# Sparse attention and expert attention on one core: loop order written by hand, against an order from a list scheduler at build time

## The chip, the cores and the metric

The kernel runs on one core of a Trainium2 chip. The metric is the time of one execution on the device in microseconds (us). A profiled execution has a span besides, from its first to its last instruction.

## The reference

Two stages follow each other, on 4 batches of 768 positions. The first is attention with 8 heads of 64, in which a position sees the last 96 positions and the first 8, with a bias by head and distance. The second takes its output x (512 features) through 4 experts, each a causal attention of its own with 64 features, and adds the two experts that a router picks for each position.

```python
# stage 1: q, k, v (4, 8, 768, 64)
scores = q @ k.T / 8 - slope[h] * dist        # dist = 96 for the 8 global columns outside the window
a = softmax(where(is_global | is_local, scores, -1e9));  x = concat_heads(a @ v)
# stage 2
logits = x @ w_gate                            # (4, 768, 4); the two largest, softmax over them: w
for e in range(4):
    ye = softmax(causal(x @ wq[e] @ (x @ wk[e]).T / 8)) @ (x @ wv[e]) @ wo[e]
    out += (e is one of the two) * w[e] * ye
```

## The kernel before

Work is cut into 24 units: 4 batches (b) by 6 row tiles of 128 positions (ri). Softmax is done without subtracting the maximum; the mask and bias of stage 1 are a factor M on the exponentials, and the sums come from a column of ones beside V. At the end a count over all reciprocals of sums decides whether a general path (a second, slow version of everything, `general_path`) has to run; with these inputs it is jumped over.

The steps of one unit u, in the order of its data:

- `load` (L274 to L282): q, k and v of the unit by three transfers on SP's queue, rows of 64 f32. `cast` (L397): q and k together, then v, to f16 on POOL.
- `transposes` (L404): 8 transposes on PE, copied out by DVE as qkT (L412). For ri = 0 POOL copies the 8 global keys into KG (L420).
- `scores1`, twice (hf = 0, 1): scores on PE (L433), exponential on ACT (L437), mask product on DVE (L439), all of 4 heads x 128 keys x (128 + 96) queries.
- `scores_g`: scores of the global keys (L449), exponential on ACT (L452). `values1`, twice: products with V and VG on PE (L460 to L468), reciprocal and scaling on DVE (L471, L474).
- `xpose`: x transposed on PE (L481), copied by DVE (L483).
- `proj_qk`: 16 matmuls (L492), copied by DVE (L494). `proj_v`: V of the experts and the gate's 4 logits in one tile (L501); V copied by ACT (L503); the router on DVE and ACT: copy of the logits, the two largest, subtraction, exponential on ACT (L511), choice, sum (L505 to L516).
- `scores2`, one to three chunks: scores on PE (L537), exponential on ACT (L540); POOL blanks the causal triangle of the first chunk (L542).
- `values2`: products on PE (L556), normalisation with the router's weights on DVE (L559 to L565). `zpose`, `output`: transposes, the product with wo on PE (L583), copy by ACT (L586), transfer to out on SP's queue (L587).

Each step runs on one fixed engine. The loop (L600 to L634) issues in pass i the steps of three units, i, i-1 and i-2, in an order written out by hand; each engine runs its own instructions in that order. Loads run three units ahead. PSUM has two tiles of two banks for scores and four of one bank for all else. Most SBUF tiles have two or three buffers.

Ahead of the loop, ACT's queue issues all transfers of weights (L291 to L296), 15 of them, with rows of 64 f32 for wq, wk and wv, and 32 of the 8 global rows of v (L300). Then POOL and DVE build masks and constants, and ACT the factors M0 and M (L333, L336). All stand on ACT's queue behind the issues.

Of the kernel before, what the change touches and what calls it, by code (L numbers as in the profile page):

```python
# [8 lines left out]
F32 = mybir.dt.float32  # L9
# [6 lines left out]
HUGE = 1.0e30  # L16
P = 128
N_G, N_L = 8, 96

# [217 lines left out]

@with_exitstack
def kernel(
# [17 lines left out]
    DV = Dh + 1  # L257

# [4 lines left out]
    ring2 = main.enter_context(tc.tile_pool(name="ring2", bufs=2))  # L263
    ring3 = main.enter_context(tc.tile_pool(name="ring3", bufs=3))
# [5 lines left out]


    raw = {}

    def load(u):  # L274
        b, ri = divmod(u, n_rt)
        rows = slice(ri * P, (ri + 1) * P)
        qk32 = ring3.tile([P, 2, H, Dh], F32, name="qk32")
        v32 = ring3.tile([P, H, Dh], F32, name="v32")
        nc.sync.dma_start(qk32[:, 0, :, :], q[b, :, rows, :].rearrange("h s d -> s h d"))
        nc.sync.dma_start(qk32[:, 1, :, :], k[b, :, rows, :].rearrange("h s d -> s h d"))  # L280
        nc.sync.dma_start(v32[:, :, :], v[b, :, rows, :].rearrange("h s d -> s h d"))
        raw[u] = (qk32, v32)  # L282

    load(0)
    load(1)


    w32 = const.tile([P, 4, nko, E, Hd], F32, name="w32")
    for n, w in enumerate((moe_wq, moe_wk, moe_wv)):
        for e in range(E):  # L290
            nc.scalar.dma_start(w32[:, n, :, e, :], w[e].rearrange("(ko kp) d -> kp ko d", kp=P))  # L291
    wo32 = const.tile([P, E // 2, Dm], F32, name="wo32")
    for p2 in range(E // 2):
        nc.scalar.dma_start(wo32[:, p2, :], moe_wo[2 * p2:2 * p2 + 2].rearrange("e d n -> (e d) n"))
    wg32 = const.tile([P, nko, E], F32, name="wg32")
    nc.scalar.dma_start(wg32[:, :, :], moe_w_gate.rearrange("(ko kp) e -> kp ko e", kp=P))  # L296
    vg32 = const.tile([N_G * H, B, Dh], F32, name="vg32")
    for b in range(B):
        for h in range(H):
            nc.scalar.dma_start(vg32[h * N_G:(h + 1) * N_G, b, :], v[b, h, 0:N_G, :])  # L300


    ident = const.tile([P, P], FH, name="ident")
    make_identity(nc, ident[:, :])


    di = const.tile([P, P + N_L], I32, name="di")
    pool.iota(di[:, 0:P], pattern=[[1, P]], channel_multiplier=-1, base=0)
    pool.iota(di[:, P:P + N_L], pattern=[[1, N_L]], channel_multiplier=-1, base=P)
    d = const.tile([P, P + N_L], F32, name="d")  # L310
    dve.tensor_copy(d[:, :], di[:, :])

    pool.affine_select(out=d[:, 0:P], in_=d[:, 0:P], pattern=[[1, P]], channel_multiplier=-1,
                       base=0, compare_op=Alu.is_ge, fill=HUGE)

    pool.affine_select(out=d[:, 0:P], in_=d[:, 0:P], pattern=[[-1, P]], channel_multiplier=1,
                       base=N_L - 1, compare_op=Alu.is_ge, fill=HUGE)
    pool.affine_select(out=d[:, P:P + N_L], in_=d[:, P:P + N_L], pattern=[[-1, N_L]],
                       channel_multiplier=1, base=N_L - 1 - P, compare_op=Alu.is_ge, fill=HUGE)

    dg = const.tile([P, P], F32, name="dg")
    pool.memset(dg[:, :], float(N_L))
    pool.affine_select(out=dg[:, :], in_=dg[:, :], pattern=[[0, P]], channel_multiplier=-1,
                       base=N_G - 1, compare_op=Alu.is_ge, fill=HUGE)
    d0 = const.tile([P, P], F32, name="d0")
    dve.tensor_tensor(d0[:, :], d[:, 0:P], dg[:, :], op=Alu.min)

# [3 lines left out]
    for h in range(H):  # L331
        hf, pr, par = h // 4, (h // 2) % 2, h % 2
        act.activation(M0[:, hf, par, pr, :], d0[:, :], func=Exp, scale=-slopes[h])  # L333
    for h in range(H):
        hf, pr, par = h // 4, (h // 2) % 2, h % 2
        act.activation(M[:, hf, par, pr, :], d[:, :], func=Exp, scale=-slopes[h])  # L336


    bm = const.tile([P, H], F32, name="bm")
    bmd = const.tile([P, H], F32, name="bmd")  # L340
    pool.memset(bmd[:, :], 0.0)

    pool.affine_select(out=bmd[:, :], in_=bmd[:, :], pattern=[[-N_G, H]], channel_multiplier=1,
                       base=0, compare_op=Alu.is_ge, fill=HUGE)
    pool.affine_select(out=bmd[:, :], in_=bmd[:, :], pattern=[[N_G, H]], channel_multiplier=-1,
                       base=N_G - 1, compare_op=Alu.is_ge, fill=HUGE)
    for h in range(H):
        dve.tensor_scalar(bm[:, h:h + 1], bmd[:, h:h + 1], -1.0, -slopes[h] * N_L,
                          op0=Alu.mult, op1=Alu.add)
    act.activation(bm[:, :], bm[:, :], func=Exp)  # L350
    VG = const.tile([P, B, H, DV], FH, name="VG")
    pool.memset(VG[:, :, :, :], 0.0)
    NL = N_G * H

    def make_vg(b):
        pool.tensor_tensor(
            VG[0:NL, b, :, 0:Dh], vg32[:, b, :].unsqueeze(1).to_broadcast([NL, H, Dh]),
            bm[0:NL, :].unsqueeze(2).to_broadcast([NL, H, Dh]), op=Alu.mult)
        pool.tensor_copy(VG[0:NL, b, :, Dh:DV], bm[0:NL, :].unsqueeze(2))

    KG = [const.tile([P, H // 2, P], FH, name=f"KG{i}") for i in range(2)]
    for t in KG:
        pool.memset(t[:, :, :], 0.0)
    NV = 4
    V1 = [const.tile([P, H, DV + 1], FH, name=f"V1_{i}") for i in range(NV)]
    for t in V1:
        pool.memset(t[:, :, Dh:DV], 1.0)
    V2 = [const.tile([P, n_rt, E, DV + 1], FH, name=f"V2_{i}") for i in range(2)]
    for t in V2:
        pool.memset(t[:, :, :, Hd:DV], 1.0)  # L370
    QK2 = [const.tile([P, n_rt, 4, P], FH, name=f"QK2_{i}") for i in range(2)]

    NA = 4
    A1 = [const.tile([P, 2, 2, 2 * P], FH, name=f"A1_{i}") for i in range(NA)]
    for t in A1:
        pool.memset(t[:, :, :, P + N_L:2 * P], 0.0)
    NLG = 4
    LG = [const.tile([P, 8], F32, name=f"LG{i}") for i in range(NLG)]
    for t in LG:
        pool.memset(t[:, E:8], -HUGE)  # L380
    rall = const.tile([P, NU, H + E], F32, name="rall")
    ones = const.tile([P, 1], F32, name="ones")
    pool.memset(ones[:, :], 1.0)

    wqk = const.tile([P, nko, 4, P], FH, name="wqk")
    wvg = const.tile([P, nko, E * Hd + E], FH, name="wvg")
    wo = const.tile([P, E // 2, Dm], FH, name="wo")
    dve.tensor_copy(wqk[:, :, 0:2, :].rearrange("p k a (e d) -> p k (a e) d", d=Hd), w32[:, 0, :, :, :])
    dve.tensor_copy(wqk[:, :, 2:4, :].rearrange("p k a (e d) -> p k (a e) d", d=Hd), w32[:, 1, :, :, :])
    act.copy(wvg[:, :, 0:E * Hd].rearrange("p k (e d) -> p k e d", d=Hd), w32[:, 2, :, :, :])  # L390
    dve.tensor_copy(wvg[:, :, E * Hd:], wg32[:, :, :])
    act.copy(wo[:, :, :], wo32[:, :, :])


    T = {}

    def cast(u):  # L397
        qk32, v32 = raw.pop(u)
        qk16 = ring2.tile([P, 2, H, Dh], FH, name="qk16")
        pool.tensor_copy(qk16[:, :, :, :], qk32[:, :, :, :])  # L400
        pool.tensor_copy(V1[u % NV][:, :, 0:Dh], v32[:, :, :])
        T[u, "qk16"] = qk16

    def transposes(u):  # L404
        b, ri = divmod(u, n_rt)
        qk16 = T.pop((u, "qk16"))
        ps = wtile([P, 2, H // 2, P], FH, "tq")
# [277 lines left out]
```

## Time and profile before

| what | value |
|---|---|
| time, median of 3 runs | 254.3 us (252.79 to 254.62) |
| profiled execution: its time | 254.38 us |
| profiled execution: its span | 252.7 us |
| mean granted clock of PE | 0.934 |
| busy: PE, DVE, ACT, POOL | 158.5, 142.8, 117.4, 69.1 us |
| transfers | 27.81 MB, mean 110 GB/s |

The span is what the profile's rows cover; 1.7 us of the execution lie around it. Busy times of an engine count overlapping instructions once. A step's row gives its engine, line, operation and the program's names for output and input; what stands in brackets behind a row is the idle time of the engine ahead of it and what ended that.

### The profile page before, as it was taken

To read this page: it belongs to the slowest core of one execution; us is meant where nothing else is said; L and a number is where in the kernel's file an instruction comes from. 1 tells how busy PE (TensorE), PEld (TensorE's weight loads), DVE (VectorE), ACT (ScalarE), POOL (GpSimd) and SP (SyncE) were. 2 spreads that over 40 slices of the span, in tenths; PEclk is the share of its full clock that TensorE was granted. 3 is DMA by queue.
4 is the path that set the end of the run, shared out by engine and by line. 5 is a ranking of instruction groups with operands and counts; after the bars stand their busy time and mean duration, and the time that the engine had idled before them with its cause. 6 is when DMAs were issued, how large, how long until landed. Compare 5 with 4: busy or idle time off the path is not lost. (4 is left out here: it accounts for less than half of the span.)

```text
span 252.7 us, 6001 instructions
## 1 busy us (share of the span) xinstructions
PE 158.5 (63%) x2362; PEld 112.2 (44%) x2362; DVE 142.8 (56%) x473; ACT 117.4 (46%) x208; POOL 69.1 (27%) x146
## 2 busy tenths in 40 slices
PE   0020000677787788789788777887878877777740
PEld 0010000545565556556656545655556645555420
DVE  0140002467677786767777687667876767674430
ACT  0000084135466756445557744466666545565510
POOL 4530009730233341332035330233242331011100
PEclk9999999999999999977999999799999979996755
DMA  8999200860654677644756557734777430111011
GB/s 157 218 245 171 49 3 1 154 97 0 159 131 99 118 166 167 145 110 87 166 129 147 119 112 169 166 93 104 143 169 166 115 96 3 43 44 45 0 42 56
DMA packets 86037, 27.81 MB, mean 110 GB/s; under 512 B 82672, under 2 KB 82672, under 8 KB 86000
## 3 DMA queue, kind: packets, MB, share of 16 engines
q1 hardware_dynamic: 78336, 25.17, 45.8%
q10 hardware_dynamic: 7664, 2.17, 4.7%
q8 instruction: 20, 0.33, 0.6%
q14 instruction: 17, 0.14, 0.2%
HBM read 21.05 MB, written 6.29 MB: 108 GB/s over the span
## 5 line engine op out<-in xcount | busy, mean ns | idle before, releaser
L437 ACT ACTIVATE A<-sc 128x896 f16<-128x896 f32 (+1 forms) x48 | 41.5, 866 | 35.9 <-PE sc L433 35.9
L439 DVE TENSOR_TENSOR A<-A,M 128x896 f16<-128x896 f16 (+1 forms) x48 | 29.8, 623 | 45.9 <-ACT A L437 45.9
L542 POOL TENSOR_SCALAR_AFFINE_SELECT A<-A 128x512 f16<-128x512 f16 x24 | 15.3, 637 | 139.8 <-ACT A L540 139.8
L540 ACT ACTIVATE A<-s 128x1024 f16<-128x1024 f32 (+1 forms) x48 | 43.3, 917 | 0.3
L410 PE MATMUL tq<-ident,qk 128*128 128x128 f16 x192 | 16.0, 231 | 42.4 <-POOL qk L400 42.4
L492 PE MATMUL pq<-xT,wqk 128*128 128x128 f16 x384 | 29.3, 237 | 4.9 <-DVE xT L483 4.8
L410 PEld LDWEIGHTS <-qk 128*128 128x128 f16 x192 | 11.7, 103 | 45.1 <-POOL qk L400 42.7
L492 PEld LDWEIGHTS <-wqk 128*128 128x128 f16 x384 | 27.0, 107 | 7.0 <-issue 5.2
L400 POOL CAST qk<-qk 128x1024 f16<-128x1024 f32 x24 | 24.9, 1036 | 0.3
L511 ACT ACTIVATE el<-dl 128x4 f32<-128x4 f32 x24 | 5.0, 207 | 37.6 <-DVE dl L509 37.6
L474 DVE TENSOR_TENSOR x<-z,rall 128x256 f16<-128x256 f32 x48 | 20.4, 424 | 1.6
L586 ACT COPY o_sb<-po 128x512 f32<-128x512 f32 x24 | 14.1, 586 | 13.9 <-PE po L583 9.3
L460 PE MATMUL z<-VG,ag 128*128 128x260 f16 x40 | 11.3, 282 | 13.9 <-ACT ag L452 13.9
L583 PE MATMUL po<-wo,zT 128*128 128x512 f16 x48 | 15.5, 405 | 6.5 <-DVE zT L575 6.5
L433 PE MATMUL sc<-qkT 64*128 64x128 f16 (+1 forms) x352 | 18.3, 226 | 1.2 <-DVE qkT L412 1.2
L412 DVE COPY qkT<-tq 128x1024 f16<-128x1024 f16 x24 | 16.4, 682 | 4.4 <-PE tq L410 4.4
L494 DVE CAST QK<-pq 128x512 f16<-128x512 f32 x24 | 16.5, 686 | 3.2 <-PE pq L492 3.2
L537 PE MATMUL s<-QK 64*128 64x128 f16 x336 | 18.2, 223 | 0.0
L481 PE MATMUL tx<-ident,x 128*128 128x128 f16 x96 | 14.4, 240 | 5.4 <-DVE x L474 5.3
L465 PE MATMUL z<-V,A 128*128 128x65 f16 x192 | 17.4, 196 | 0.0
L556 PE MATMUL z<-V,A 128*128 128x65 f16 x336 | 16.0, 201 | 1.3 <-ACT A L540 1.2
L333 ACT ACT_TABLE_LOAD x1 | 1.3, 1283 | 32.6 <-DMA vg<-in_v_dram 32.6
(73 smaller groups left out, 262.9 us busy)
## 6 DMA issues: line engine op xcount, KB each, us to landing
qk<-in_q_dram SPq DMA_DIRECT2D x24, 256.0 KB
qk<-in_k_dram SPq DMA_DIRECT2D x24, 256.0 KB
v<-in_v_dram SPq DMA_DIRECT2D x24, 256.0 KB
out_dram<-o_sb SPq DMA_DIRECT2D x24, 256.0 KB
w<-in_moe_wq_dram ACTq DMA_DIRECT2D x4, 128.0 KB
w<-in_moe_wk_dram ACTq DMA_DIRECT2D x4, 128.0 KB
w<-in_moe_wv_dram ACTq DMA_DIRECT2D x4, 128.0 KB
wo<-in_moe_wo_dram ACTq DMA_DIRECT2D x2, 256.0 KB
```

Source lines behind the costliest of these rows:

```text
L400: pool.tensor_copy(qk16[:, :, :, :], qk32[:, :, :, :])
L410: nc.tensor.transpose(ps[:, s, p, :], qk16[:, s, 2 * p:2 * p + 2, :], ident[:, :])
L412: dve.tensor_copy(qkT[:, :, :, :], ps[:, :, :, :])
L433: mm(o, lhsT=kt[L, 1, p, :], rhs=qkT[L, 0, p, 0:N_L] if prev else qkT[L, 0, p, :], start=True, stop=True)
L437: act.activation(A[:, :, :, 0:w], sc[:, :, :, 0:w], func=Exp, scale=scale1)
L439: dve.tensor_tensor(A[:, :, :, 0:w], A[:, :, :, 0:w], m, op=Alu.mult)
L465: mm(z[:, h % 4, :], lhsT=A[:, par, pr, 0:P], rhs=V1[u % NV][:, h, 0:DV], start=not ri, stop=not ri)
L474: dve.tensor_tensor(T[u, "x16"][:, 4 * hf:4 * hf + 4, :], z[:, :, 0:Dh], r.unsqueeze(2).to_broadcast([P, 4, Dh]), op=Alu.mult)
L492: mm(ps[:, j, :], lhsT=wqk[:, ko, j, :], rhs=xT[:, ko, :], start=(ko == 0), stop=(ko == nko - 1))
L494: dve.tensor_copy(QK2[b % 2][:, ri, :, :], ps[:, :, :])
L537: mm(sc[:, par, n, :], lhsT=qk[L, ki, 2 + p2, :], rhs=qk[L, ri, p2, :], start=True, stop=True)
L540: act.activation(A2[:, :, 4 * c:4 * c + m, :], sc[:, :, 0:m, :], func=Exp, scale=scale2)
```

## The change

The steps stay much as they are, but are cut into pieces, each with a list of the engines that may run it and a length on each of them (in us, constants in the text), the pieces it has to wait for, and a rank: 5.0 us (`PACE`) times the unit plus its place in the unit. At build time a list scheduler (`Stream.run`) takes again and again the piece that can start first by these lengths, the lower rank first among equals, with 0.25 us against every engine but the first in its list, and issues it on the engine found. Pieces with a choice: the casts of unit 0's k (DVE), the memsets, the copies of QK, V and the output (DVE or ACT), the weight casts, and the mask product (DVE or POOL). All SBUF tiles of the loop have three or more buffers, most of them four (`R`).

All transfers, the weights' and the output's too, are pieces issued by SP in the scheduler's order. Weights are read with four rows of w per partition, 1 KB in a piece, so features lie at kp * 4 + ko; x is transposed with a step of 4 columns to match. The global rows of v come by 8 transfers instead of 32. The gate's columns stand twice in the weights: the maximum of 8 then gives each logit twice, and its third value is the second largest. The exponential of the logits is taken without subtracting the maximum, straight from PSUM, and the sum comes from the choosing instruction's accumulator; its reciprocal is taken there. The count at the end has the router's sums too, and the general path is the side of the branch that jumps.

```diff
+class Stream:
+    def __init__(self, kinds):
+        self.free = {"PE": 0.0, "ACT": 0.0, "DVE": 0.0, "POOL": 0.0, "DMA": 0.0}
+        self.tail = {"PE": 0.22, "ACT": 0.13, "DVE": 0.13, "POOL": 0.15, "DMA": 2.0}
...
+    def run(self):
+        left = dict.fromkeys(self.ops)
+        while left:
+            best = None
+            for key in left:
+                t = self.ready(key)
+                if t is None:
+                    continue
+                for n, (e, length) in enumerate(self.ops[key][1].items()):
+                    start = max(t, self.free[e] + self.turn(e, self.ops[key][4]))
+                    c = (start + (0.25 if n else 0.0), self.ops[key][3], n, start, key, e, length)
+                    if best is None or c[:3] < best[:3]:
+                        best = c
...
+            self.free[e] = start + length
+            self.done[key] = start + length + self.tail[e]
+            del left[key]
+            fn(e)
...
-            nc.scalar.dma_start(w32[:, n, :, e, :], w[e].rearrange("(ko kp) d -> kp ko d", kp=P))
+        st.add(("ld", "qkv"[n]), ld(w32[:, n, :, :, :].rearrange("p e k d -> p e (k d)"),
+                                   w.rearrange("e (kp ko) d -> kp e (ko d)", ko=nko)),
+               {"DMA": 1.7}, rank=(1.0, 1.5, 6.0)[n])
...
-            nc.scalar.dma_start(vg32[h * N_G:(h + 1) * N_G, b, :], v[b, h, 0:N_G, :])
+            nc.sync.dma_start(vg32[h * N_G:(h + 1) * N_G, :, :],
+                              v[:, h, 0:N_G, :].rearrange("b g d -> g b d"))
...
+            add("ld" + "qkv"[n], load(n, src), {"DMA": 1.2}, [("c" + "qkv"[n], u - R)], -1.0 + 0.1 * n)
...
+                {"POOL": 0.53} if u else ({"POOL": 0.53}, {"DVE": 0.4})[n],
...
+            add(f"x{hf}", x1, {"ACT": 0.86 if ri else 0.54}, [f"s{hf}", (f"z{hf}", u - R), c("A1zero")],
+                3.5 + 0.5 * hf)
+            add(f"m{hf}", m1, {"DVE": 0.56 if ri else 0.35, "POOL": 1.9 if ri else 1.1},
+                [f"x{hf}", c(("M", 1 if ri else 0, hf))], 4.0 + 0.5 * hf)
...
+            xv = x16[i][:, :].rearrange("p (kp ko) -> p ko kp", ko=nko)
...
+        add("eqk", lambda e: copy(e, QK2[b % 2][:, ri, :, :], T.pop(("pq", u))[:, :, :]), {"DVE": 0.62, "ACT": 0.55},
+            ["pq"] + free2, 8.0)
...
-        dve.tensor_copy(lg[:, 0:E], ps[:, E * Hd:])
-        mx = ring2.tile([P, 8], F32, name="mx")
-        dve.max(mx[:, :], lg[:, :])
-        dl = ring2.tile([P, E], F32, name="dl")
-        dve.tensor_scalar(dl[:, :], lg[:, 0:E], mx[:, 0:1], None, op0=Alu.subtract)
...
+        add("xr", lambda e: act.activation(el[i][:, :], T["pv", u][:, lg0:lg0 + E], func=Exp),
+            {"ACT": 0.12}, ["pv", ("wr", u - R)], 8.5)
+
+        def wr_(e):
+            ps = T["pv", u]
+            dve.max(mx[i][:, :], ps[:, lg0:lg0 + 2 * E])
+            dve.scalar_tensor_tensor(wr[i][:, :], ps[:, lg0:lg0 + E], mx[i][:, 2:3], el[i][:, :],
+                                     op0=Alu.is_ge, op1=Alu.mult, accum_out=zall[:, u:u + 1])
+            dve.reciprocal(zi[i][:, :], zall[:, u:u + 1])
...
+        add("eo", lambda e: copy(e, o_sb[i][:, :], T.pop(("po", u))[:, :]), {"ACT": 0.52, "DVE": 0.62},
+            ["po", ("so", u - R)], 13.0)
+        add("so", lambda e: nc.sync.dma_start(out[b, rows, :], o_sb[i][:, :]), {"DMA": 0.7}, ["eo"], 13.0)
...
-        for i in range(NU + 2):
...
+        st.run()
     main.close()
     n_good = nc.values_load(flag_i[0:1, 0:1])
-    with tc.If(n_good < P * NU * (H + E)):
+    with tc.If(n_good < P * NU * (H + E + 1), preferred_fallthrough_block=False):
         general_path(tc, q, k, v, moe_w_gate, moe_wq, moe_wk, moe_wv, moe_wo, out)
```

## Rows read from the trace of the kernel before

**Rows 1.** The page's busy times: us, share of the span, instructions.
```profile
PE 158.5 (63%) x2362; PEld 112.2 (44%) x2362; DVE 142.8 (56%) x473; ACT 117.4 (46%) x208; POOL 69.1 (27%) x146
```
**Rows 2.** Timeline of the start: start us, us, engine, line, operation.
```profile
16.90 15.70 ACTq L300 DMA_DIRECT2D vg<-in_v_dram  x32
32.62 1.28 ACT L333 ACT_TABLE_LOAD   x1 [32.62 <-DMA vg<-in_v_dram]
39.76 1.07 ACT L437 ACTIVATE A<-sc 128x512 f16<-128x512 f32 x2
```
**Rows 3.** Timeline of ACT: the first exponentials of units 3 and 23.
```profile
64.63 0.92 ACT L437 ACTIVATE A<-sc 128x896 f16<-128x896 f32 x1 [0.50 <-PE sc L433]
...
223.44 0.92 ACT L437 ACTIVATE A<-sc 128x896 f16<-128x896 f32 x1 [0.40 <-PE sc L433]
```
**Rows 4.** The end: timeline of ACT, and PE's branch by line (ns min/median/max).
```profile
245.01 0.59 ACT L586 COPY o_sb<-po 128x512 f32<-128x512 f32 x1 [4.33 <-issue]
...
L648 PEldq COMPARE_BRANCH  x1: 3962/3962/3962, 245.9 to 245.9; - x1
```
**Rows 5.** One loop pass by windows: busy us of each engine (instructions), clock, DMA share, GB/s.
```profile
64.16:72.03 7.87, 6.05 (x96) 4.27 (x94) 5.73 (x19) 4.50 (x8) 2.16 (x4) 1.00 0.57 135
```
**Rows 6.** Timeline of one loop pass.
```profile
152.90 0.92 ACT L437 ACTIVATE A<-sc 128x896 f16<-128x896 f32 x1 [0.65 <-PE sc L433]
...
155.96 0.21 ACT L511 ACTIVATE el<-dl 128x4 f32<-128x4 f32 x1 [1.88 <-DVE dl L509]
...
156.39 0.28 PE L460 MATMUL z<-VG,ag 128*128 128x260 f16 x1 [0.72 <-ACT ag L452]
...
159.01 0.42 DVE L483 COPY xT<-tx 128x512 f16<-128x512 f16 x1 [0.49 <-PE tx L481]
```
**Rows 7.** The page's DMA queues (q1 SP's, q10 ACT's): packets, MB, share.
```profile
q1 hardware_dynamic: 78336, 25.17, 45.8%
q10 hardware_dynamic: 7664, 2.17, 4.7%
```
**Rows 8.** A window of the start, columns as in rows 5.
```profile
4.00:8.00 4.00, 0.00 (x0) 0.00 (x0) 0.00 (x0) 0.00 (x0) 0.00 (x0) 1.00 1.35 226
```
**Rows 9.** Groups by line and shape: busy us, mean ns of one, idle before.
```profile
L494 DVE CAST QK<-pq 128x512 f16<-128x512 f32 x24 | 16.5, 686 | 3.2 <-PE pq L492 3.2
L586 ACT COPY o_sb<-po 128x512 f32<-128x512 f32 x24 | 14.1, 586 | 13.9 <-PE po L583 9.3 <-issue 4.3
L503 ACT CAST V<-pv 128x256 f16<-128x256 f32 x24 | 8.9, 372 | 7.8 <-PE pv L501 7.3
L509 DVE TENSOR_SCALAR dl<-LG,mx 128x4 f32<-128x4 f32 x24 | 5.5, 229 | 0.8
L516 DVE TENSOR_REDUCE zr<-wr 128x1 f32<-128x4 f32 x24 | 3.8, 157 | 0.8
L505 DVE COPY LG<-pv 128x4 f32<-128x4 f32 x24 | 3.6, 151 | 0.3 <-ACT V L503 0.3
L641 DVE DVE_READ_ACCUMULATOR ge<-rall,ge 128x1 f32 x1 | 0.1, 84 | 0.0
```
**Rows 10.** Timeline: mask products beside POOL's work, in passes 0 and 6.
```profile
40.32 1.04 POOL L356 TENSOR_TENSOR VG<-vg,bm 64x512 f16<-64x512 f32 x1
40.38 1.60 DVE L439 TENSOR_TENSOR A<-A,M 128x512 f16<-128x512 f16 x2 [18.34 <-ACT A L437]
...
88.17 1.04 POOL L400 CAST qk<-qk 128x1024 f16<-128x1024 f32 x1
88.85 0.64 DVE L439 TENSOR_TENSOR A<-A,M 128x512 f16<-128x512 f16 x1 [0.50 <-ACT A L437]
...
90.34 0.42 DVE L439 TENSOR_TENSOR A<-A,M 128x512 f16<-128x512 f16 x1 [0.16 <-ACT A L437]
```
**Rows 11.** Two windows in passes 8 and 9, columns as in rows 5.
```profile
107.00:109.00 2.00, 0.87 (x16) 0.67 (x17) 1.56 (x7) 1.01 (x3) 0.00 (x0) 1.00 0.65 115
...
111.00:115.00 4.00, 3.97 (x45) 3.26 (x45) 1.88 (x4) 1.84 (x2) 0.52 (x1) 0.50 0.92 213
```

More of the change, by code (lines that the diff above doesn't have):

```diff
@@ L235, in general_path, with add, turn, ready @@
             dma(out[bass.ds(b, 1), ri * P:(ri + 1) * P, :].rearrange("b s d -> (b s) d"), o_sb[:, :])
+class Stream:
+    def __init__(self, kinds):
+        self.free = {"PE": 0.0, "ACT": 0.0, "DVE": 0.0, "POOL": 0.0, "DMA": 0.0}
+        self.tail = {"PE": 0.22, "ACT": 0.13, "DVE": 0.13, "POOL": 0.15, "DMA": 2.0}
+        self.kinds = {k: (n, []) for k, n in kinds.items()}
+        self.rows = False
+        self.ops, self.done = {}, {}
+    def add(self, key, fn, engines, after=(), rank=0.0, kind=None, until=()):
+        assert key not in self.ops, key
+        self.ops[key] = (fn, engines, tuple(after), rank, kind, tuple(until))
+    def turn(self, e, kind):
+        return 0.1 if e == "PE" and (kind == "s") != self.rows else 0.0
+    def ready(self, key):
+        fn, engines, after, rank, kind, until = self.ops[key]
+        t = 0.0
+        for a in after:
+            if a not in self.done:
+                return None
+            t = max(t, self.done[a])
+        if kind:
+            for r in until:
+                if any(a not in self.done for a in self.ops[r][2] if a != key and a not in until):
+                    return None
+            n, taken = self.kinds[kind]
+            if len(taken) >= n:
+                for a in taken[-n]:
+                    if a not in self.done:
+                        return None
+                    t = max(t, self.done[a])
+        return t
+    def run(self):
[11 more added lines that the diff above has]
+                        best = c
+            assert best, list(left)[:20]
+            start, key, e, length = best[3:]
+            fn, engines, after, rank, kind, until = self.ops[key]
+            if kind:
+                self.kinds[kind][1].append(until)
+            if e == "PE":
+                self.rows = kind == "s"
+            self.free[e] = start + length
+            self.done[key] = start + length + self.tail[e]
+            del left[key]
+            fn(e)
@@ L284, with stile, ring, copy @@
[L284 to L290, printed above, removed]
-            nc.scalar.dma_start(w32[:, n, :, e, :], w[e].rearrange("(ko kp) d -> kp ko d", kp=P))
+    def stile(shape, name):
+        return psS.tile(shape, F32, name=name, tag="s")
+    def ring(n, shape, dt, name):
+        return [const.tile(shape, dt, name=f"{name}_{i}") for i in range(n)]
+    def copy(e, o, i):
+        act.copy(o, i) if e == "ACT" else (dve if e == "DVE" else pool).tensor_copy(o, i)
@@ L361 @@
[L361 to L371, printed above, removed]
@@ new lines, in c_dg, with c_factor, fn @@
+    def c_dg(e):
+        pool.memset(dg[:, :], float(N_L))
+        pool.affine_select(out=dg[:, :], in_=dg[:, :], pattern=[[0, P]], channel_multiplier=-1,
+                           base=N_G - 1, compare_op=Alu.is_ge, fill=HUGE)
+    def c_factor(first, hf):
+        def fn(e):
+            for h in range(4 * hf, 4 * hf + 4):
+                t, s = (M0, d0) if first else (M, d)
+                act.activation(t[:, hf, h % 2, (h // 2) % 2, :], s[:, :], func=Exp, scale=-slopes[h])
+        return fn
@@ new lines, in fill, with fn @@
+    def fill(views, value):
+        def fn(e):
+            for t in views:
+                eng[e].memset(t, value)
+        return fn
+    st.add("ident", lambda e: make_identity(nc, ident[:, :]), {"POOL": 0.7}, rank=-9)
+    st.add("iota", c_iota, {"POOL": 0.45}, rank=-8)
+    st.add("d", lambda e: dve.tensor_copy(d[:, :], di[:, :]), {"DVE": 0.3}, ["iota"], rank=-8)
+    st.add("mask", c_mask, {"POOL": 0.9}, ["d"], rank=-8)
+    st.add("dg", c_dg, {"POOL": 0.45}, rank=-7)
+    st.add("d0", lambda e: dve.tensor_tensor(d0[:, :], d[:, 0:P], dg[:, :], op=Alu.min),
+           {"DVE": 0.3}, ["mask", "dg"], rank=-7)
@@ new lines @@
+    for hf in range(2):
+        st.add(("M", 0, hf), c_factor(True, hf), {"ACT": 0.9}, ["d0"], rank=-6)
+        st.add(("M", 1, hf), c_factor(False, hf), {"ACT": 1.2}, ["mask"], rank=2.0)
+    st.add("bmd", c_bm, {"POOL": 1.0}, rank=4.0)
+    st.add("bm", lambda e: act.activation(bm[:, :], bm[:, :], func=Exp, scale=-1.0), {"ACT": 0.15},
+           ["bmd"], rank=4.0)
+    st.add("VG0", fill([VG[:, :, :, :]], 0.0), {"DVE": 1.2, "POOL": 1.9}, rank=4.0)
+    st.add("KG0", fill([t[:, :, :] for t in KG], 0.0), {"DVE": 0.7, "POOL": 1.1}, rank=2.0)
@@ new lines, with cast_w, wv_view @@
+    st.add(("ld", "vg"), ld_vg, {"DMA": 1.5}, rank=5.5)
+    def cast_w(o, i):
+        return lambda e: copy(e, o, i)
+    def wv_view(t):
+        return t.rearrange("p k (e d) -> p k e d", d=Hd)
+    for n, o in (("q", wqk[:, :, 0:2, :].rearrange("p k a (e d) -> p k (a e) d", d=Hd)),
+                 ("k", wqk[:, :, 2:4, :].rearrange("p k a (e d) -> p k (a e) d", d=Hd)),
+                 ("v", wv_view(wvg[:, :, 0:E * Hd]))):
+        st.add(("w", n), cast_w(o, w32[:, "qkv".index(n), :, :, :].rearrange("p e k d -> p k e d")),
+               {"DVE": 1.1, "ACT": 1.1}, [("ld", n)], rank=7.0)
@@ new lines, with inside, fn @@
+    for u in range(NU):
+        unit(u)
+    good = const.tile([P, 3], F32, name="good")
+    ge = const.tile([P, NU * (H + E)], F32, name="ge")
+    def inside(t, n, lo, hi, col):
+        def fn(e):
+            dve.tensor_scalar(ge[:, 0:n], t, lo, None, op0=Alu.is_ge)
+            dve.scalar_tensor_tensor(ge[:, 0:n], t, hi, ge[:, 0:n], op0=Alu.is_le, op1=Alu.mult,
+                                     accum_out=good[:, col:col + 1])
+        return fn
+    last = NU - 1
+    flat = rall[:, 0:last, :].rearrange("p u n -> p (u n)")
```

550 lines of the change are left out of this document (263 added, 287 removed).

## The prediction

> **What bounds the kernel now.** I read the page's busy times first, then the timeline of the start, the sums of one loop pass, and the same pass in order of time. No engine is near full: the busiest compute engines stand at 63% and 56% of the span [rows 1]. The reader should see three stages. The first 39.8 us hold almost no work. ACT issues 47 small transfers itself, the last 32 of them from 16.9 to 32.6 us; only then comes its table load, and the first exponential of scores starts at 39.76 [rows 2]. The loop follows: the first exponential of unit 3 starts at 64.63 and that of unit 23 at 223.44 [rows 3], so 158.8 us for 20 units, 7.94 us a unit. From there to the end of the last output copy are 22.2 us [rows 3, 4], and to the span's end 7.1 more. The span is 252.7 us, the execution's own time 254.38; those 1.7 us lie around it, and the median of the runs is 254.3.
>
> A pass of 7.87 us has 6.05 us of PE, 5.73 of DVE, 4.50 of ACT and 2.16 of POOL, at full clock [rows 5]: it is not bound by any one of them. In order of time it is one chain that crosses the engines once a pass [rows 6]: second exponential of scores at 152.90, then behind its mask product on DVE the whole normalisation of an older unit, then the router's copy, maximum and subtraction, so that ACT stands still for 1.88 us until 155.96 and holds the global scores behind it; values1 on PE can only then start (156.39), and the transposed x is copied at 159.01, 8 us after the same copy of the pass before. The order of the loop makes this chain, not the data.
>
> **The start.** The change takes the 47 issues from ACT. SP issues q, k, v of unit 0, then wq and wk, then unit 1, the small v rows, wv and the gate, unit 2, wo, unit 3. Until unit 3 has landed these are 12 transfers of 128 x 512 f32 and 2.17 MB of weights, 5.3 MB [rows 7]; at the 226 GB/s that the DMA engines reached in the same stretch [rows 8] 23.5 us, from about 3 us: 26.5. The rows of 1 KB matter only here. Packets of the two queues cost nearly the same time each (4.7% of the span for 7664, 45.8% for 78336), so fewer packets would cut the weights' 11.9 us (4.7% of 252.7) to some 3, and if it goes by bytes nothing is saved: 17.5 to 26.5 us, and I take the upper end, since the rate is that of a measured stretch. With half of the cast, transposes, copy and scores behind it, 2.5 us, the first exponential of unit 3 starts at 29, against 64.63: 35.6 us gained. ACT's other constants are no longer behind transfers. What is late next is the load itself, some 7 us a unit until unit 3, so the engines' order barely matters there.
>
> **The steady pace.** The list scheduler interleaves two to three units and has buffers of 4, so the chain of [rows 6] is cut, and what remains is work per unit.
> - Router: copy, subtraction and sum go from DVE (0.151, 0.229, 0.157), an accumulator read of 0.084 comes [rows 9]: 0.45 less. The exponential no longer waits for them. Doubling the gate widens one projection by 4 columns of 260 and costs nothing that shows; the maximum now reads PSUM, at most some 0.1 more.
> - DVE and ACT together: 5.73 + 4.50 - 0.45 = 9.8 us. The copies of QK (0.686), V (0.372) and the output (0.586) [rows 9], 1.6 us, may go to either of the two, so the scheduler can level them.
> - POOL may take mask products. Its two-input product of 512 columns took 1.04 us [rows 10], so 896 columns are 1.8 us by the same rate, against 0.6 on DVE. It is chosen where DVE is booked 0.25 us longer than POOL; I take one of the two products of a unit. POOL then has 4.0 us, DVE and ACT 9.2, or 4.6 each.
> - Against this: a mask product that meets a POOL operation is longer. With a cast beside it the 512-column product took 0.64 us, alone 0.42; beside the product on POOL two took 1.60 in place of 0.84 [rows 10], so 0.2 to 0.8 us a meeting. Two DVE operations of a unit (the product that stays, the weighting of the experts) have both inputs in SBUF; POOL is busy for two thirds of the time; 2 x 0.68 x 0.4 = 0.55. DVE is at 5.15 us.
> - PE at 6.05 counts the fill of each group of matmuls, which overlaps when groups follow closely; I take it below DVE. The x transposes now load columns with a step of 4 elements, which no row shows: 0, or at most a doubled load, 4 x 0.1 us a unit. I take 0, because PE has that room.
> - DMA: 45.8% of 252.7 us is 115.7, or 4.8 us a unit with its output [rows 7]. SP waits for an output copy with loads queued behind it, but these run four units ahead, 20 us and more; if that lead were lost, a load's own 4 us would show in each unit.
>
> How much of the time the busiest engine is filled is not known: 100% gives 5.15 us, the fill of now (5.73 of 7.87, 73%) gives 7.1. I take the middle, 87%: 5.9 us.
>
> On the product beside POOL the Trainium skill (SBUF — State Buffer, Who interferes with whom) says that a DVE instruction with two SBUF inputs and a GpSimd instruction that reads SBUF exclude each other, and that the second to start blocks for the whole of the first. By that rule, against my mean, a meeting with a 1.8 us product on POOL would cost up to 1.8 us; the 1.60 us pair agrees with it, since its first product ended only behind POOL's.
>
> **The end.** From unit 23's first exponential to its output's end: not above the 22.2 us of now; one unit's work laid end to end is 6.05 + 5.73 + 4.50 = 16.3 [rows 5], of which its two halves overlap, while rests of unit 22 come between. I take 16.5, with 13 to 22. The final branch now has its other side in the fall-through place. PE's branch lasted 3.96 us [rows 4] while the last output still had to land, so 0 to 2.6 us are saved; I take 2: 5.1 us.
>
> **The sum.** 29 + 20 x 5.9 + 16.5 + 5.1 = 168.6, and 1.7 around the span: 170.3, so 170 us.
>
> **The rivals.**
> 1. Pace of 6.5 to 7.5 us: DVE and POOL hold each other, and an order fixed from costs that are a tenth too low (it books 0.62 for the QK copy of 0.686) lets engines wait in turn. For it: the 1.60 us pair; POOL goes from 2.2 to 4 us a unit. Against: four buffers of each kind. 182 to 202 us. Worked out: with every meeting at 0.8 us DVE has 4.6 + 2 x 0.68 x 0.8 = 5.7, and filled to 80% a unit takes 7.1: 194 us. The rule named above works in this direction.
> 2. Pace of 4.9 to 5.3, with the transfers' 4.8 us as floor: 150 to 158. For it: four resources are near 4.7; against: four that are equal rarely all stay full.
> 3. Slower than before: the clock. Behind 2 us in which PE was busy for 0.87 the granted clock stood at 0.50, and PE was then busy for 3.97 of 4 us [rows 11]. If the new order left the clock there throughout, the 4.6 us that I put PE's net work at would be 9.2, with gaps 9.8 a unit: 29 becomes 37, and 37 + 196 + 18 + 5.1 + 1.7 = 258. It decides from a pace of 9.7. Against: the low clock followed thin stretches, and the new order makes PE denser.
> 4. The change doesn't do what it says: the order keeps the old chain's pace of 7.9, and the start alone is gained: 29 + 158 + 22 + 7 + 1.7 = 218.
>
> **How the numbers follow.** Forecast (pace 5.4 to 6.4, 160 to 181) 0.53; rival 2 0.17; rival 1 0.24; rival 4 0.03; rival 3 0.03. The start is sure within 9 us, the pace moves the sum by 20 us for each us. From 154 to 192 leaves out half of rival 2, the upper half of rival 1's range and rivals 3 and 4, about 2 in 10. Within 1% is what a measurement of this kernel cannot tell from no change; no case lies there, and 0.01 stands for the unforeseen: faster 0.96, same 0.01, slower 0.03.
>
> **What would show it.** Start right: the first exponential of scores before 10 us, unit 3's near 29. Pace right: 118 us from there to unit 23's, DVE busy for 85 to 90% of a unit's time. Rival 1: mask products and casts on POOL well above their lengths of now, DVE waiting on them. Rival 2: DMA share above 0.9 through the middle. Rival 3: granted clock of half in most slices. Router right: no wait of ACT on DVE of 1.9 us a unit. End: no long branch on PE. I would be wrong most likely by the fill, a number for which the profile gives only the two ends.

## The result, and the profile after

The changed kernel takes 180.5 us (median of 4, 179.41 to 181.15), the kernel before 253.6 on the same chip (252.55 to 254.62): a ratio of 0.7115, 95% interval 0.7064 to 0.7165. The profiled execution took 180.74 us with a span of 179.0. The forecast was 170, its range 154 to 192.

The page of the changed kernel, busy times, granted clock by slices, transfers by slices, SP's queue and the last chain by engine:

```profile
PE 139.7 (78%) x2366; PEld 109.7 (61%) x2366; DVE 138.6 (77%) x438; ACT 110.2 (62%) x203; POOL 93.3 (52%) x169
...
PEclk9999669999999999999999999999999999999855
DMA  5996995999799599979899999910101031011120
...
q1 hardware_dynamic: 80656, 27.34, 67.6%
...
DVE 44%; PE 34%; DMA 6%; ACT 4%; issue 3%; SPq 3%; ACTq 0%; DVEq 0%
```

Against [rows 1] DVE does nearly the same work in 74 us less time, PE is busy for 19 us less and POOL for 24 more. The chain hops between DVE and PE nearly all the way, and the loads end after about two thirds of the span (the tenths fall to 0 and 1), long before the work that needs them.

The timeline of ACT: the first exponential of all, that of unit 3, the four of units 22 and 23 in one row, and the output copies behind them (start us, us, then as in [rows 3]):

```profile
8.05 1.06 ACT L590 ACTIVATE A<-sc 128x512 f16<-128x512 f32 x2
...
30.42 1.73 ACT L590 ACTIVATE A<-sc 128x896 f16<-128x896 f32 x2 [0.64 <-PE sc L583]
...
144.10 3.35 ACT L590 ACTIVATE A<-sc 128x896 f16<-128x896 f32 x4
...
149.66 0.59 ACT L347 COPY o_sb<-po 128x512 f32<-128x512 f32 x1 [2.04 <-issue]
...
157.56 0.59 ACT L347 COPY o_sb<-po 128x512 f32<-128x512 f32 x1 [1.39 <-issue]
...
163.51 0.59 ACT L347 COPY o_sb<-po 128x512 f32<-128x512 f32 x1 [0.32 <-PE po L749]
...
167.32 0.59 ACT L347 COPY o_sb<-po 128x512 f32<-128x512 f32 x1 [0.46 <-ACT A L704]
170.86 0.59 ACT L347 COPY o_sb<-po 128x512 f32<-128x512 f32 x1 [2.95 <-PE po L749]
```

These rows hold the forecast's milestones. Unit 3 begins at 30.42, against 64.63 [rows 3]. Unit 23 begins two exponentials into the row of four, at 145.7, so 20 units take 115.3 us, 5.76 each (7.94 before). From there to the last copy's end at 171.45 are 25.7 us (22.2 before), and 7.55 more to the span's end (7.1 before). Five of the 24 output copies are still to come when unit 23 begins; in the kernel before it was three.

Windows of the changed kernel, columns as in [rows 5]:

```profile
30.00:150.00 120.00, 105.52 (x1884) 84.25 (x1885) 105.73 (x317) 83.77 (x148) 71.94 (x113) 1.00 0.77 170
...
80.00:90.00 10.00, 9.57 (x174) 7.42 (x173) 8.99 (x29) 8.20 (x14) 6.87 (x17) 1.00 0.95 224
...
130.00:140.00 10.00, 9.64 (x191) 8.65 (x190) 7.55 (x29) 7.16 (x16) 1.28 (x2) 1.00 0.08 29
...
160.00:170.00 10.00, 6.86 (x123) 4.39 (x122) 5.56 (x27) 7.12 (x11) 1.59 (x3) 0.95 0.15 55
```

PE and DVE are both busy for 88% of the 120 us. In single stretches PE is the fuller one, at 96%, also where the transfers are done and POOL has little to do (130 to 140). These windows do not say which of the two sets the pace; experiments 4 and 5 were made for that.

The groups by line and shape that answer to [rows 9, 10]:

```profile
L595 DVE TENSOR_TENSOR A<-A,M 128x896 f16<-128x896 f16 x31 | 22.2, 727 | 2.7 <-ACT A L590 2.6
...
L595 POOL TENSOR_TENSOR A<-A,M 128x896 f16<-128x896 f16 x9 | 17.6, 1952 | 5.2 <-ACT A L590 4.9
...
L347 DVE CAST QK<-pq 128x512 f16<-128x512 f32 x21 | 14.4, 686 | 6.9 <-PE pq L659 6.7
...
L731 DVE SCALAR_TENSOR_TENSOR cw<-wr,zi,rall 128x4 f32<-128x4 f32 x24 | 10.0, 415 | 0.9
...
L678 ACT ACTIVATE el<-pv 128x4 f32<-128x4 f32 x24 | 4.5, 187 | 2.2 <-DVE V L347 2.2
...
L595 POOL TENSOR_TENSOR A<-A,M 128x512 f16<-128x512 f16 x2 | 2.3, 1152 | 0.1
```

POOL got 11 of the 48 mask products, not 24. The little weighting of the experts, cw, on 4 columns, rose from 222 ns in the kernel before to a mean of 415 (its median is 224, so a few long ones make the mean). The router's exponential has lost its waits (1.88 us in the pass of [rows 6], 37.6 us in all): it stands 2.2 us in all. One meeting of DVE and POOL in the timeline shows what became of cw:

```profile
31.40 1.92 DVE L731 SCALAR_TENSOR_TENSOR cw<-wr,zi,rall 128x4 f32<-128x4 f32 x1
31.42 1.88 POOL L595 TENSOR_TENSOR A<-A,M 128x896 f16<-128x896 f16 x1 [0.37 <-ACT A L590]
...
33.35 0.42 DVE L733 TENSOR_TENSOR z<-z,cw 128x256 f16<-128x256 f32 x1
...
33.83 0.28 PE L744 MATMUL tz<-ident,z 128*128 128x128 f16 x2 [2.31 <-DVE z L733]
```

An operation on 4 columns takes 1.92 us because it ends only with POOL's product, and PE, whose next instruction needs what follows, stands for 2.31 us. A second pair agrees (1.19 us beside 1.15, at 54.8 us), and without products on POOL the longest cw is 0.62 us (experiment 2). A meeting costs up to POOL's whole instruction, 1.7 us more, where the forecast took a mean of 0.4. The rule of the Trainium skill that the forecast weighed (SBUF — State Buffer, Who interferes with whom) agrees with these rows in what such a meeting costs; which of the two was first they do not tell, since cw's record starts 0.02 us ahead of POOL's.

### The profile page after: what moved, and what is told of

Read it like the earlier page. It is cut to its first block, busy times and chain, and to the rows that moved or that the text cites. A ratio compares the mean times of both kernels' runs of the same rounds, so it can differ in the third digit from the quotient of the medians.

```text
span 179.0 us, 5965 instructions
## 1 busy us (share of the span) xinstructions
PE 139.7 (78%) x2366; PEld 109.7 (61%) x2366; DVE 138.6 (77%) x438; ACT 110.2 (62%) x203; POOL 93.3 (52%) x169
## 3 DMA queue, kind: packets, MB, share of 16 engines
q1 hardware_dynamic: 80656, 27.34, 67.6%
## 4 chain that ended last, share of the span: by engine, by line
DVE 44%; PE 34%; DMA 6%; ACT 4%; issue 3%; SPq 3%; ACTq 0%; DVEq 0%
DVE A L595 10%; PE pq L659 8%; DVE x L617 5%; DVE cw L731 5%; DVE qkT L347 5%; DVE z L733 4%; PE po L749 4%; PE pv L665 4%; DMA raw<-in_v_dram 4%; PE z L724 3%; DVE QK L347 3%; PE s L700 3%; PE tx L649 3%; DMA w<-in_moe_wv_dram 2%; SPq L537 2%
## 5 line engine op out<-in xcount | busy, mean ns | idle before, releaser
L347 POOL CAST qk<-raw 128x512 f16<-128x512 f32 x47 | 30.9, 670 | 15.8 <-DMA raw<-in_k_dram 8.0
L595 DVE TENSOR_TENSOR A<-A,M 128x896 f16<-128x896 f16 (+1 forms) x37 | 26.1, 719 | 2.8 <-ACT A L590 2.6
L595 POOL TENSOR_TENSOR A<-A,M 128x896 f16<-128x896 f16 (+1 forms) x11 | 19.9, 1806 | 5.3 <-ACT A L590 4.9
L347 POOL CAST V<-raw 128x512 f16<-128x512 f32 x24 | 15.3, 642 | 11.7 <-PE z L609 8.3
L606 PE MATMUL z<-V,A 128*128 128x65 f16 x192 | 17.5, 197 | 2.6 <-DVE A L595 1.6
L347 ACT COPY o_sb<-po 128x512 f32<-128x512 f32 x18 | 10.6, 588 | 12.9 <-PE po L749 8.9
L347 ACT CAST V<-pv 128x256 f16<-128x256 f32 x23 | 8.6, 376 | 15.5 <-PE pv L665 15.4
L606 PEld LDWEIGHTS <-A 128*128 128x128 f16 x192 | 14.3, 100 | 6.0 <-DVE A L595 2.6
L583 PE MATMUL sc<-qkT 64*128 64x128 f16 x192 | 14.6, 223 | 2.5 <-ACT A L590 1.2
L665 PE MATMUL pv<-wvg,xT 128*128 128x264 f16 x96 | 15.5, 286 | 1.0 <-DVE wvg L347 1.0
```

Of the source, the lines that this page charges most:

```text
L347: act.copy(o, i) if e == "ACT" else (dve if e == "DVE" else pool).tensor_copy(o, i)
L595: eng[e].tensor_tensor(a, a, M[:, hf, :, :, :] if ri else M0[:, hf, :, :, :], op=Alu.mult)
L606: mm(z[:, h % 4, :], lhsT=a[:, par, pr, 0:P], rhs=V1[u % (R + 1)][:, h, 0:DV], start=not ri, stop=not ri)
L665: mm(ps[:, :], lhsT=xT[i][:, ko, :], rhs=wvg[:, ko, :], start=(ko == 0), stop=(ko == nko - 1))
```

## The experiments

All ratios are to the kernel before, run beside it (medians 252.5 to 253.1 us). "The changed kernel" is 0.7115, 180.5 us.

**1. The start alone, in the kernel before.** SP issues the weights behind load 0, still in rows of 256 B, and the small v rows in 8 transfers; the loop is untouched.

```diff
     load(0)
-    load(1)
...
+        if n == 2:
+            load(1)
-            nc.scalar.dma_start(w32[:, n, :, e, :], w[e].rearrange("(ko kp) d -> kp ko d", kp=P))
+            nc.sync.dma_start(w32[:, n, :, e, :], w[e].rearrange("(ko kp) d -> kp ko d", kp=P))
...
-            nc.scalar.dma_start(vg32[h * N_G:(h + 1) * N_G, b, :], v[b, h, 0:N_G, :])
+        nc.sync.dma_start(vg32[h * N_G:(h + 1) * N_G, :, :], v[:, h, 0:N_G, :].rearrange("b g d -> g b d"))
```

> The kernel before with its hand-written order; only the issue of the weights and of the global rows of v goes from ACT's queue to SP's (8 transfers for the global rows instead of 32, rows of 256 bytes kept), behind the load of unit 0. Theory (the start is worth what ACT's 47 issues cost, and no more): the first exponential of scores at 9 to 12 us instead of 39.8, that of unit 3 near 35 instead of 64.6, the pace unchanged at 7.9 us a unit, 222 to 230 us. Rival (the loads then take the time instead, because the weights stand in front of units 1 to 3 on the one queue): unit 3 at 42 us or later, 232 to 245 us.

233.7 us, ratio 0.926 (0.917 to 0.936), in the rival's range. Its timeline of ACT, the first exponentials of units 3 and 23:

```profile
47.66 0.92 ACT L437 ACTIVATE A<-sc 128x896 f16<-128x896 f32 x1 [0.57 <-PE sc L433]
...
205.80 0.92 ACT L437 ACTIVATE A<-sc 128x896 f16<-128x896 f32 x1 [0.41 <-PE sc L433]
```

That is 7.91 us a unit, the old pace. So of the 34 us by which unit 3 begins earlier, moving the issues gives 17; the rest comes with the new order and the wider rows, which no run separates. Its timeline of POOL shows what is late next:

```profile
8.14 0.61 POOL L401 CAST V<-v 128x512 f16<-128x512 f32 x1
21.17 1.04 POOL L356 TENSOR_TENSOR VG<-vg,bm 64x512 f16<-64x512 f32 x1 [12.41 <-DMA vg<-in_v_dram]
...
26.92 1.04 POOL L400 CAST qk<-qk 128x1024 f16<-128x1024 f32 x1
```

POOL stands 12.41 us before the small v rows, with the casts of units 1 to 3 queued behind; in the changed kernel the casts of unit 1 begin at 11.35, ahead of the first of these products at 14.93. The page gives this run's queue 85808 packets and 55.2% of 232.3 us, 128.2 us of 16 engines; the changed kernel has 80656 and 121.0. So the wider rows take 7.2 us from the transfers' summed time, between the forecast's nothing and 9.

**2. The mask product on POOL.** None there, then one of two by force:

```diff
-            add(f"m{hf}", m1, {"DVE": 0.56 if ri else 0.35, "POOL": 1.9 if ri else 1.1},
+            add(f"m{hf}", m1, {"DVE": 0.56 if ri else 0.35},
...
+            add(f"m{hf}", m1, ({"DVE": 0.56 if ri else 0.35}, {"POOL": 1.9 if ri else 1.1})[hf],
```

> The changed kernel with the mask product on DVE alone (48 of 48, instead of 37 and 11 on POOL). Theory A (DVE stands still beside a product on POOL, and loses there what it is spared): no operation of DVE above 1.3 us, the weighting of the experts back from 415 to near 225 ns on average, DVE's busy time about the same, 175 to 181 us. Rival (relieving DVE by 11 products of 0.6 us is worth its price): 185 to 190 us.

> The changed kernel with the second mask product of each unit always on POOL (24 instead of 11). Theory A (each product on POOL holds DVE up when DVE comes to an operation with two SBUF inputs): DVE operations of 1.5 to 2 us about twice as often as in the changed kernel, 184 to 195 us. Rival (DVE is the bound and is relieved): 172 to 178 us.

None: 179.3 us, 0.710 (0.702 to 0.718). All of hf = 1: 192.2, 0.757 (0.747 to 0.767). Both lie in the ranges of theory A. The groups of the first, then those of the second:

```profile
L595 DVE TENSOR_TENSOR A<-A,M 128x896 f16<-128x896 f16 x40 | 26.2, 671 | 3.9 <-ACT A L590 3.8
...
L731 DVE SCALAR_TENSOR_TENSOR cw<-wr,zi,rall 128x4 f32<-128x4 f32 x24 | 6.4, 268 | 0.8
```

```profile
L595 POOL TENSOR_TENSOR A<-A,M 128x896 f16<-128x896 f16 x20 | 39.3, 1976 | 10.5 <-ACT A L590 10.3
...
L595 DVE TENSOR_TENSOR A<-A,M 128x896 f16<-128x896 f16 x20 | 19.3, 971 | 9.7 <-ACT A L590 9.7
...
L731 DVE SCALAR_TENSOR_TENSOR cw<-wr,zi,rall 128x4 f32<-128x4 f32 x24 | 11.0, 458 | 0.9
```

With half of the products gone from DVE, those that stay take 971 ns in place of 671 and cw 458 in place of 268. DVE is busy for 139.5 us with 24 on POOL, 138.6 with 11 and 136.4 with none: the relief is eaten by the meetings. The split of this piece between the engines, a main part of the forecast's DVE sum, buys nothing. How much of the 12 us that 24 products cost comes of the meetings is not shown, since the order is another one too.

**3. How much hangs on the order alone.** The length of one piece is told as 0.01 us more; no work changes.

```diff
-            T.pop(("pq", u))[:, :, :]), {"DVE": 0.62, "ACT": 0.55}
+            T.pop(("pq", u))[:, :, :]), {"DVE": 0.63, "ACT": 0.55}
```

> A control: the changed kernel with one length of the scheduler raised from 0.62 to 0.63 us (the copy of QK on DVE), which does the same work in another order. If the time hangs on how much work each engine has, it stays within 2 us of 180.5; if it hangs on the particular order, it may move by 4 us or more either way, and differences of that size between other orders prove nothing.

184.3 us (181.6 to 186.2), 0.732 (0.724 to 0.741). But the 181.6 us had a mean granted clock of 0.966, and the three executions above 184 us had 0.928 to 0.946; the changed kernel's four had 0.952 to 0.968. At like clocks (0.965 and 0.966) the changed kernel took 180.3 us, so the new order is 1.3 us longer, within the scatter of either kernel. Whether the low clock comes of the order is not shown, and this run does not settle what an order is worth; experiments 5, 6 and 8 say more. It does show that 0.01 us make another order: unit 23 begins at 141.5 us, not 145.7, and the end behind it takes 31.0 us, not 25.7.

**4. A dose on DVE, and on PE, with the scheduler told of it.** A second copy of the transposed x out of PSUM on DVE, into a tile that nobody reads; half of the QK projection computed twice on PE.

```diff
+            copy(e, junk[:, :, :], ps[:, :, :])
-        add("ex", ..., {"DVE": 0.35},
+        add("ex", ..., {"DVE": 0.7},
```

```diff
-            for j in range(4):
+            for j in (0, 1, 0, 1, 2, 3):
-        add("pq", pq, {"PE": 0.9},
+        add("pq", pq, {"PE": 1.35},
```

> The changed kernel with a second copy of each transposed x by DVE into an unused tile (some 0.35 us more a unit, the scheduler told of it). Theory (DVE's work, at 85 to 90% fill, sets the pace): 24 x 0.35 / 0.87 = 9.6 us more, 188 to 192 us. Rival (the pace is set by waits across engines or by PE): 180 to 184 us.

> The changed kernel with 8 of the 16 matmuls of the QK projection done twice (some 0.45 us more PE a unit, the scheduler told of it). Theory (DVE sets the pace, PE has room): 181 to 184 us. Rival (PE is as full as DVE, its chain through the projections is on the path): 10 us more or above, 189 to 193 us.

DVE: 190.5 us, 0.759 (0.750 to 0.767). PE: 198.3, 0.787 (0.778 to 0.795), 17.8 more for 10.8 of work. The first number is what a bound by DVE gives; the second is more than the work that was added. Both had another order as well, so neither settles it.

**5. The same doses, with the lengths left as they were.** The order is then the changed kernel's own, and only the work is added.

> The same 8 extra matmuls a unit on PE as in the PE dose before, but the scheduler is still told 0.9 us, so its order is that of the changed kernel, instruction for instruction, and only the work is added. By the clean rows a unit's pq piece grows by half, some 0.45 us, 10.8 us in all. If PE is as full as DVE: 187 to 192 us. If PE is below DVE, as the forecast took it, and the first dose's 17.8 us came of the changed order: 180 to 184 us. If PE alone bounds the pace and the work is dearer than the rows say: 195 or more, as in the first dose.

> The same extra copy a unit on DVE (0.35 us by the clean row, 8.4 us in all) as in the DVE dose before, with the order of the changed kernel kept. If DVE's work sets the pace, nearly all of it comes out: 187 to 190 us. If the first dose's 10 us came mostly of the changed order: 181 to 184 us.

PE: 187.8 us (187.78 to 188.11), 0.744 (0.740 to 0.749). DVE: 181.9 us (180.41 to 182.98), 0.722 (0.717 to 0.727). The first exponential of unit 3, the last output copy and the window of 30 to 150 us, first of the PE dose, then of the DVE dose:

```profile
29.64 1.73 ACT L590 ACTIVATE A<-sc 128x896 f16<-128x896 f32 x2 [0.64 <-PE sc L583]
...
177.78 0.59 ACT L347 COPY o_sb<-po 128x512 f32<-128x512 f32 x1 [2.77 <-PE po L749]
...
30.00:150.00 120.00, 109.12 (x1945) 89.74 (x1944) 99.43 (x302) 79.23 (x142) 69.15 (x112) 0.99 0.77 165
```

```profile
28.63 1.73 ACT L591 ACTIVATE A<-sc 128x896 f16<-128x896 f32 x2 [0.64 <-PE sc L584]
...
170.17 0.59 ACT L347 COPY o_sb<-po 128x512 f32<-128x512 f32 x1 [2.41 <-PE po L755]
...
30.00:150.00 120.00, 105.67 (x1873) 84.07 (x1874) 109.05 (x333) 82.87 (x149) 69.57 (x111) 1.00 0.75 166
```

Of PE's 10.8 us 7.3 come out, of DVE's 8.4 only 1.4. From unit 3's first exponential to the last copy's end the changed kernel takes 141.0 us, the PE dose 148.7 and the DVE dose 142.1. By the pages' busy times the doses were smaller, 8.9 us on PE (148.6 for 139.7) and 5.8 on DVE (144.4 for 138.6). So PE's work, at this place, sets the pace two thirds of the way or more, and DVE's hardly: the forecast's "I take it below DVE" is refuted. Told and untold, the same work took 198.3 and 187.8 us on PE, 190.5 and 181.9 on DVE: 10.5 and 8.6 us come with the order, in part through the clock (0.917 to 0.956 in the told runs, 0.963 to 0.986 in the untold ones). One limit: the copy stands just ahead of DVE's wait for the projection, and filled it (that wait falls from 6.7 to 3.3 us), so a dose elsewhere on DVE may cost more; that was not tried.

**6. Fewer units in flight.** With twice the rank per unit the older unit goes first (loads keep their ranks).

```diff
-PACE = 5.0
+PACE = 10.0
```

> The changed kernel with ranks of 10 us a unit instead of 5 for all but the loads, so that pieces of older units go first where several could start. Theory (the 25 us from unit 23's first exponential to the end are work of four units in flight, not idle time; moving it earlier moves the first exponential later): the first exponential of unit 23 later by 3 to 8 us, the end that much shorter behind it, 178 to 183 us. Rival (units in flight cost time at the end): 170 to 175 us.

192.7 us, 0.766 (0.760 to 0.773). Its timeline of ACT, the two exponentials of unit 23 in stage 1 and the last output copy:

```profile
165.48 0.92 ACT L590 ACTIVATE A<-sc 128x896 f16<-128x896 f32 x1
...
167.19 0.92 ACT L590 ACTIVATE A<-sc 128x896 f16<-128x896 f32 x1 [0.62 <-PE sc L583]
...
182.84 0.59 ACT L347 COPY o_sb<-po 128x512 f32<-128x512 f32 x1 [3.64 <-issue]
```

The end is now 18 us from unit 23's first exponential, close to the 16.5 of the forecast, but the pace is 6.8 us a unit, in part by the clock (0.94 in the window of 30 to 150 us, 1.00 in the changed kernel). Both theories missed the total. What the end depends on shows when one counts, in each run with the scheduler, the output copies that come after unit 23's first exponential: with three of them the end is 17.2 to 18.0 us (this run, the told DVE dose, the measured lengths of experiment 8), with four 21.2 and 21.6, with five 25.1 to 26.9 (six runs), with six 31.0 (experiment 3). In three orders of the same work (experiment 3, the changed kernel, this run) the shorter end comes with the slower pace: 5.6, 5.8 and 6.8 us a unit with ends of 31.0, 25.7 and 18.0.

**7. The branch laid out as before.**

```diff
-    with tc.If(n_good < P * NU * (H + E + 1), preferred_fallthrough_block=False):
+    with tc.If(n_good < P * NU * (H + E + 1)):
```

> The changed kernel with the branch at the end laid out as before the change. Theory (the layout saves nothing: PE's branch lasts 3.6 us in the changed kernel against 4.0 before): from the end of the last output copy to the span's end 7 to 8 us, 180 to 181 us. Rival (the layout saves some 2 us elsewhere): 182 to 183 us.

178.7 us, 0.712 (0.706 to 0.719). The branch's line in the changed kernel (ns min/median/max, first and last start us), and then the last output copy and the branch's line in this one:

```profile
L796 PEldq COMPARE_BRANCH  x2: 95/1834/3573, 170.4 to 171.0; - x2
...
L796 SPq COMPARE_BRANCH  x2: 37/45/53, 172.4 to 175.0; - x2
```

```profile
169.39 0.59 ACT L347 COPY o_sb<-po 128x512 f32<-128x512 f32 x1 [2.41 <-PE po L749]
...
L796 PEldq COMPARE_BRANCH  x1: 3522/3522/3522, 169.4 to 169.4; - x1
...
L796 SPq COMPARE_BRANCH  x1: 45/45/45, 170.9 to 170.9; - x1
```

PE's long branch is there in both; the new layout adds a second branch on each engine, SP's at 175.0. From the last copy's end to the span's end are 5.5 us here (the span is 175.5) and 7.55 in the changed kernel. The other runs of the changed kernel agree: 7.4 to 8.5 us in the eight that keep the new layout (experiments 2 to 6), 5.9 and 5.6 in the two below. So in the traces the layout costs 2 us, and gives none. Neither expectation had this. The whole times alone would not show it: the ratios are 0.712 and 0.7115, the kernel before having taken 252.5 us beside this run and 253.6 beside the changed kernel.

**8. Both undone, and lengths as measured.** No product on POOL and the branch as before; then also DVE's lengths as the trace of the changed kernel shows them from start to start.

```diff
-            add(f"n{hf}", n1, {"DVE": 0.45},
+            add(f"n{hf}", n1, {"DVE": 0.55},
-        add("wr", wr_, {"DVE": 0.42},
+        add("wr", wr_, {"DVE": 0.55},
-        add("n2", n2, {"DVE": 0.6},
+        add("n2", n2, {"DVE": 0.8},
```

> All mask products on DVE and the branch's layout as before, together. If the two effects are what they looked like one by one (1.3 and 1.8 us) and add up: 177 to 178 us. If one or both were scatter: 179 to 181 us.

> As the kernel with both undone, with three lengths of DVE's pieces told to the scheduler as the trace of the changed kernel shows them from start to start (normalisation 1 0.55 for 0.45 us, router 0.55 for 0.42, normalisation 2 0.80 for 0.60; 0.53 us a unit that the planner did not know of). The work is the same, only the order differs. If waits that a misjudged length plans in are what keeps DVE at 88 per cent: 170 to 175 us. If the order is a matter of chance, as the control with 0.01 us more showed: anywhere from 175 to 184 us, with no lean to the better side.

Both undone: 176.7 us (175.41 to 177.84), 0.700 (0.694 to 0.706), the fastest version of the study, 3.8 us under the changed kernel; the two effects add up, to a little more than the first expectation had. Measured lengths: 180.1 us (179.25 to 181.55), 0.712 (0.707 to 0.718), worse by 3.4 than the same work with wrong lengths. Better lengths do not make the better order here. The clock has a part, as two windows of the run with measured lengths show:

```profile
100.00:104.00 4.00, 2.24 (x50) 1.45 (x48) 4.00 (x9) 4.00 (x7) 1.58 (x3) 1.00 0.89 227
104.00:108.00 4.00, 4.00 (x39) 3.05 (x36) 2.56 (x5) 2.49 (x5) 0.00 (x0) 0.57 1.03 249
```

DVE and ACT were busy for all of 4 us while PE was busy for 2.24, and in the 4 us behind that the granted clock was 0.57, mostly its lower level of 1.2 GHz, with PE busy all the time on 39 matmuls.

## Why the prediction was right, and by which steps not

The time was in the range, 10 us over the forecast. Its sum against the profiled execution: start 29 and 30.4; 20 units 118 and 115.3; end 16.5 and 25.7; tail (from the last copy's end to the span's end) 5.1 and 7.55.

- **Start: right.** First exponential at 8.05, unit 3's 1.4 us late. The transfers' term held: POOL's casts of unit 3 wait for its q, k and v until 25.33, 26.14 and 27.00, where the sum has 26.5, and from 3 to 26.5 us the transfers ran at 227 GB/s for the 226 taken. That is the end of the range at which wider rows save nothing, though in summed time they take 7.2 us less; why the stretch is no shorter for it, no run shows. Moving the issues gave half of the gain by itself (experiment 1).
- **Pace: right in size, by a wrong cause and some luck.** 5.76 for 5.9, DVE 88% full for 87%; the 87% were only the middle between two ends. PE is as full as DVE, and the dose that comes out is PE's. The step "PE ... I take it below DVE", with a net 4.6 us a unit, was mis-sized: 105.5 us in 120 are 5.1 for each 5.76. The 4.6 us that levelling was to leave DVE leaned on 24 products on POOL; there were 11, and they were worth nothing. The copies were not levelled either: by the window, DVE has 5.1 us a unit and ACT 4.0, for 4.6 each. That DVE still comes near the forecast's 5.15 is luck.
- **The mask product beside POOL: mis-sized.** 0.4 us taken for a meeting, up to 1.7 measured; 1.8 us was the forecast's figure by the rule of the Trainium skill that stood beside it (SBUF — State Buffer, Who interferes with whom), and these rows bear it out. That this did not throw the time out is luck too: the scheduler put only 11 products on POOL; with 24 the second run of experiment 2 shows 192 us, within the first rival's range.
- **End: the largest miss, 9.2 us.** "One unit's work laid end to end, with rests of unit 22 between" left out how many units the scheduler has unfinished when unit 23 starts: five output copies are still to come, and experiment 6 shows the end growing by 4 to 5 us with each. Most tiles of the loop have four buffers (KG, QK2 and V2, which serve a whole batch, have two, which the section on the change passes over). Pace and end have to be read as one: from unit 3's first exponential to the last copy 134.5 us were forecast and 141.0 came, an error of 6.5 us; experiment 6 moves time between the two and loses in sum.
- **Tail: wrong in sign.** 2 us of gain were taken; PE's branch stayed at 3.6 us, and the new layout lost 2 us (experiment 7). With the layout of before the tail is 5.5 to 5.9 us, over 1 us less than the 7.1 of the kernel before; PE's branch starts there 0.6 us ahead of the last copy's end, and 0.3 us behind it in the kernel before.
- **Router: right.** ACT's wait for DVE is 2.2 us in all. The strided transposes of x load in 113 ns each (median; 98 before), 0.06 us a unit, the lower end.
- **Rivals.** The transfer floor did not decide: the last three loads are issued at 111 to 113 us, 33 us before unit 23 begins. The clock fell only in places: the changed kernel's slices of 6 stand at 18 to 27 us; PE was busy for 0.99 of the 2 us before them, and for 1.00 of the next 2, in which the granted clock was already 0.70. In the profiles of experiment 7 and of the DVE dose of experiment 5, with the same order and no such slices, unit 3 began 1.8 us earlier, at 28.7 and 28.6. The old chain is gone. A slip in the chances: what 154 to 192 us leaves out adds up to 0.085 + 0.12 + 0.06, nearer 3 in 10 than 2.

What stays open: which order is good. Four pairs of runs with the same work in two orders differ by 3.4, 8.6, 10.5 and 12.2 us (experiments 8, 5, 5 and 6), the clock having a part in each, and no rule was found that says which way. Open is also how the 2.2 us a unit that the pace gained divide among the new order, the deeper buffers and the shorter router: no run has one of them without the others.

## What to carry to other kernels

In a kernel whose order is computed from lengths, test a suspected bound by adding work without telling the planner; told, the order changes, and that can move the time as much as the work. Read pace and end together: each unit that is begun early and still unfinished when the last one starts lengthens the end. Before a piece is given to a second engine, look at what the first engine's smallest instructions cost beside it.

## What the hardware showed that was not expected

An operation on 128 x 4 numbers took 1.92 us beside a product of 1.88 us on POOL, 0.22 alone. A product of 896 columns took POOL 1.95 to 1.98 us on average, where 1.8 were worked out from the narrower one. And placing the long path out of the way of the branch made the end 2 us longer, with a second branch on each engine; what fills the 4.0 us from SP's second branch (175.0) to the span's end is not shown.
